# Pre, post, F1 and F2 of a fused attention and feed-forward kernel moved into two 64-row tiles of TensorE, where QK already runs

## The chip, the cores and the metric

One core of a Trainium2 chip. Times are device microseconds; quoted times are medians of the runs of one kernel. The profile is one execution with the hardware profiler on; its span is some microseconds shorter than the device time, as it runs from the first to the last instruction. Here a run is called slow when it took over 1.5% longer than the fastest of its kernel. Engines: PE is TensorE (PEld its weight loads), DVE is VectorE, ACT is ScalarE, POOL is GpSimd, SP is SyncE.

## The reference

```python
batch, n_heads, seq, head_dim = (8, 12, 448, 64)
n_tokens, d_model, d_ff = (3584, 768, 2048)

scores = scale * np.matmul(q, k.transpose(0, 1, 3, 2))           # QK
scores = np.einsum('bhij,hg->bgij', scores, w_pre)               # pre: mixes the 12 heads
scores = scores - np.max(scores, axis=-1, keepdims=True)
attn = np.exp(scores)
attn = attn / (np.sum(attn, axis=-1, keepdims=True) + 1e-09)
attn = np.einsum('bhij,hg->bgij', attn, w_post)                  # post: mixes the heads again
out = np.matmul(attn, v)                                         # AV
x = out.transpose(0, 2, 1, 3).reshape(3584, 768)
h = np.maximum(x @ w_in, 0.0)                                    # F1
return h * h @ w_out                                             # F2
```

## The kernel before

The kernel is a program that plans itself: when it is built, a list scheduler walks over "units" of TensorE work (T, the transposes of q and k; QK, pre, post, AV, F1, F2), picks the next one by priority among those whose inputs and banks of PSUM (TensorE's output memory) are free by durations written into the code, and assigns the copies out of PSUM to ACT or DVE. What comes out is a fixed order for each engine with semaphore waits between them. On the chip nothing is chosen any more.

The heads are mixed in chunks of 10 query positions x 12 heads = 120 rows. `pre` multiplies a chunk of scores by a block-diagonal 120 x 120 matrix; ACT takes exp; `post` multiplies by the block-diagonal matrix of `w_post`, whose rows are first scaled by one over the row sum (reciprocal on DVE, "fold" on POOL).

```python
# pre: one matmul, K = 120, one bank
eng.matmul(ps[0:128, bank, 0:S], wk1[:, :], dring[:, slot, :], start=True, stop=True)

# post: four matmuls of 120 columns, K = 120, one bank
for jb in range(RJ):
    eng.matmul(ps[0:128, bank, jb * NR:(jb + 1) * NR],
               pring[:, pr, jb * JB:jb * JB + 128], wk2s[:, ws, :], start=True, stop=True)
# ... the copy out: runs of CH = 10 elements
src = ps[0:JB, bank, 0:RJ * NR].rearrange("p (a k n) -> p a k n", a=RJ, k=H)
return copy(eng, en, a2t[half][:, :, :, cs * CH:(cs + 1) * CH], src)

# F1: a chain of 6 matmuls, K = 128, into one bank; F2 likewise with 16
for ft in range(f0, f0 + 3):
    eng.matmul(ps[:, bank, 0:n], w_in_sb[:, ft, t16 * 128:(t16 + 1) * 128],
               xt[:, ft, c0:c1], start=(ft == 0), stop=(ft == NFT - 1))

# priorities of the units (lower goes first): AV 1, post 2, pre 3, QK 4, T 5, F1 6, F2 7
```

QK alone runs in two 64-row tiles at once: TensorE's 128 rows are used as two halves, each with weights and a matmul of its own (here two heads of 64 dimensions, each into its own bank). There are 8 PSUM banks. F1 of a batch needs that batch's AV and the F2 of the batch before; F2 needs all of F1. So F work is the filler between pieces of attention work.

The softmax here doesn't subtract the row's maximum and nothing guards it: scores larger than these inputs give would overflow.

## Time and profile before

| | before |
|---|---|
| time | 600.76 us (600.68 to 600.85, 2 runs) |
| span of the profile, granted clock | 595.2 us, 0.999 |
| matmuls | 6024 |
| busy PE, ACT, DVE, POOL | 98, 75, 59, 58% |
| PE runs out of inputs | about 10 us in all |

Three more lines of the page of the kernel before matter later: the two groups of copies of post's output (DVE and ACT; busy us, then the mean ns of one; the column after that is idle time before them), and the granted clock in 40 slices (9 is 90% or more).

```profile
L388 DVE CAST a2t<-ps 112x480 bf16<-112x480 f32 x195 | 124.7, 650 | 45.5 <-PE ps L877 43.6
L387 ACT ACTIVATE a2t<-ps 112x480 bf16<-112x480 f32 x165 | 92.6, 576 | 24.5 <-PE ps L877 22.6
```

```profile
PEclk9999999999999999999999999999999999999999
```

### The profile page before, as it was taken

The page shows a single profiled execution, that of the slowest core. Times are in us where ns is not written, and L with a number is a line of the kernel's source. Part 1 is how long each engine was busy: PE and PEld are TensorE (multiplying, and loading weights), DVE is VectorE, ACT ScalarE, POOL GpSimd, SP SyncE. Part 2 cuts the span into 40 slices and gives each one's busy share as a digit, 9 for nine tenths or more (in the row PEclk, how much of TensorE's full clock was granted, in tenths as well). Part 3 has the DMA queues.
Part 4 walks back from the last instruction along what each step waited for, and adds up shares of the span by engine and source line. Part 5 has one row for each costly group of instructions (what it writes and reads, how often), then busy time and mean ns, then how long its engine had stood idle before and what let it go on. Part 6 is the DMA issues. An engine that isn't in the chain of part 4 may idle for free.

```text
span 595.2 us, 15926 instructions
## 1 busy us (share of the span) xinstructions
PE 580.4 (98%) x6024; PEld 377.4 (63%) x6024; DVE 351.5 (59%) x899; ACT 446.4 (75%) x1160; POOL 342.3 (58%) x684
## 2 busy tenths in 40 slices
PE   7989999999999999999999999999999999999997
PEld 3656766685876565656556655657555665566974
DVE  4778775587666755754768655765647535230420
ACT  2779577888777979797977797889788867772531
POOL 8786758377692657645764566474367534761001
PEclk9999999999999999999999999999999999999999
DMA  9999879577886986459744896447544565301103
GB/s 135 184 225 214 141 132 202 114 144 116 153 135 129 180 157 133 88 91 170 162 88 72 163 183 146 77 81 124 132 100 81 91 116 131 82 2 49 34 26 80
DMA packets 95851, 72.40 MB, mean 122 GB/s; under 512 B 6192, under 2 KB 93440, under 8 KB 95776
## 3 DMA queue, kind: packets, MB, share of 16 engines
q0 software_dynamic: 49504, 33.43, 36.5%
q1 hardware_dynamic: 46128, 37.85, 29.1%
q8 instruction: 49, 0.80, 0.5%
q14 instruction: 26, 0.21, 0.1%
q10 hardware_dynamic: 144, 0.10, 0.1%
HBM read 45.70 MB, written 11.01 MB: 95 GB/s over the span
## 4 chain that ended last, share of the span: by engine, by line
PE 88%; ACT 3%; DMA 3%; DVE 2%; POOL 1%; SPq 1%; issue 1%; ACTq 0%; POOLq 0%
PE ps L1080 24%; PE ps L998 24%; PE ps L877 12%; PE ps L813 11%; PE ps L939 7%; PE ps L738 7%; PE ps L612 3%; ACT stage L387 2%; DMA dring<-stage 2%; DMA kraw<-in_k_dram 1%; SPq L785 1%; ACT pring L831 1%; DVE w_out_sb L656 1%; DVE stage L388 1%; DVE a2t L388 0%
## 5 line engine op out<-in xcount | busy, mean ns | idle before, releaser
L831 ACT ACTIVATE pring<-ps 120x448 bf16<-120x448 f32 x360 | 191.2, 557 | 15.9 <-PE ps L813 13.1
L847 POOL TENSOR_SCALAR wk2s<-wk2b,rinv 120x120 bf16<-120x120 bf16 x350 | 125.1, 367 | 84.4 <-DVE rinv L841 81.7
L998 PE MATMUL ps<-xt,w_in_sb 128*128 128x448 bf16 (+6 forms) x1248 | 173.4, 281 | 0.2 <-DVE h1t L1027 0.2
L1080 PE MATMUL ps<-w_out_sb,h2t 128*128 128x384 bf16 x896 | 165.1, 326 | 0.0
L388 DVE CAST a2t<-ps 112x480 bf16<-112x480 f32 x195 | 124.7, 650 | 45.5 <-PE ps L877 43.6
L1036 POOL TENSOR_TENSOR h2t<-h1t 128x448 bf16<-128x448 bf16 (+6 forms) x176 | 114.0, 661 | 43.7 <-ACT h1t L1026 23.6
L998 PEld LDWEIGHTS ps<-xt,w_in_sb 128*128 128x128 bf16 x1248 | 98.9, 97 | 41.1 <-issue 5.7
L877 PE MATMUL ps<-wk2s,pring 120*128 120x120 bf16 x1440 | 119.3, 216 | 1.6 <-POOL wk2s L847 0.5
L877 PEld LDWEIGHTS ps<-wk2s,pring 120*128 120x128 bf16 x1440 | 93.5, 97 | 42.3 <-POOL wk2s L847 5.0
L1080 PEld LDWEIGHTS ps<-w_out_sb,h2t 128*128 128x128 bf16 x896 | 83.3, 97 | 56.5 <-issue 6.3
L387 ACT ACTIVATE a2t<-ps 112x480 bf16<-112x480 f32 x165 | 92.6, 576 | 24.5 <-PE ps L877 22.6
L841 DVE RECIPROCAL rinv<-rowsum 120x1 f32<-120x1 f32 x360 | 53.3, 157 | 93.2 <-ACT pring L831 92.5
L387 ACT ACTIVATE stage<-ps 120x896 bf16<-120x896 f32 (+3 forms) x99 | 88.9, 918 | 23.5 <-PE ps L738 23.1
L388 DVE CAST stage<-ps 120x896 bf16<-120x896 f32 (+2 forms) x87 | 93.6, 1086 | 20.2 <-PE ps L738 19.4
L813 PE MATMUL ps<-dring,wk 120*128 120x448 bf16 x350 | 93.8, 353 | 2.8 <-ACT pring L831 1.6
L1141 POOL DMA_DIRECT2D out_dram<-osb x54 | 34.1, 634 | 84.1 <-ACT osb L387 72.1
L831 ACT ACTIVATION_READ_ACCUMULATOR pring<-ps 120x1 f32 x360 | 79.9, 222 | 0.0
L1027 DVE TENSOR_SCALAR h1t<-ps 128x448 bf16<-128x448 f32 (+6 forms) x111 | 43.7, 396 | 31.3 <-PE ps L998 25.0
L1026 ACT ACTIVATE h1t<-ps 128x448 bf16<-128x448 f32 (+5 forms) x97 | 42.7, 443 | 20.4 <-PE ps L998 19.7
L738 PE MATMUL ps<-qkt 64*128 64x448 bf16 (+2 forms) x372 | 54.7, 359 | 1.5 <-ACT stage L387 0.5
L813 PEld LDWEIGHTS ps<-dring,wk 120*128 120x128 bf16 x350 | 32.5, 97 | 27.0 <-ACT pring L831 2.9
L387 ACT ACTIVATE osb<-ps 128x384 f32<-128x384 f32 x35 | 17.2, 491 | 35.6 <-PE ps L1080 35.0
(41 smaller groups left out, 352.5 us busy)
## 6 DMA issues: line engine op xcount, KB each, us to landing
dring<-stage SPq DMA_DIRECT2D x342, 105.0 KB
vraw<-in_v_dram POOLq DMA_DIRECT2D x24, 224.0 KB, 6.0
qraw<-in_q_dram POOLq DMA_DIRECT2D x23, 224.0 KB, 6.4
kraw<-in_k_dram POOLq DMA_DIRECT2D x23, 224.0 KB, 7.9
w_in_sb<-in_moe_w_in_dram POOLq DMA_DIRECT2D x8, 384.0 KB, 10.7
w_out_sb<-in_moe_w_out_dram POOLq DMA_DIRECT2D x12, 256.0 KB, 33.2
out_dram<-osb POOLq DMA_DIRECT2D x8, 336.0 KB, 3.6
out_dram<-osb POOLq DMA_DIRECT2D x8, 288.0 KB, 4.2
```

Of the source, the lines that this page charges most:

```text
L387: return eng.activation(o, i_, AF.Copy)
L388: return eng.tensor_copy(o, i_)
L738: r_ = eng.matmul(ps[0:m, banks[par], 0:S], qkt[r0:r0 + 64, pb, p, 0, i0:i0 + m], qkt[r0:r0 + 64, pb, p, 1, :], start=True, stop=True,)
L813: return eng.matmul(ps[0:128, bank, 0:S], wk1[:, :], dring[:, slot, :], start=True, stop=True)
L831: return eng.activation(pring[:, pr, 0:S], ps[0:NR, bank, 0:S], AF.Exp, accum_out=rowsum[:, pr, :])
L841: return eng.reciprocal(rinv[:, pr, :], rowsum[:, pr, :])
L847: return eng.tensor_scalar(wk2s[:, ws, :], wk2b[:, :, :].rearrange("p a b -> p (a b)"), rinv[:, pr, :], 1.0, op0=ALU.mult, op1=ALU.mult)
L877: r_ = eng.matmul(ps[0:128, bank, jb * NR:(jb + 1) * NR], pring[:, pr, jb * JB:jb * JB + 128], wk2s[:, ws, :], start=True, stop=True,)
L998: r_ = eng.matmul(ps[:, bank, 0:n], w_in_sb[:, ft, t16 * 128:(t16 + 1) * 128], xt[:, ft, c0:c1], start=(ft == 0), stop=(ft == NFT - 1),)
L1027: return eng.tensor_scalar(h1t[:, s, 0:n], ps[:, bank, 0:n], 0.0, None, op0=ALU.max)
L1036: return eng.tensor_tensor(h2t[:, t16, o0:o0 + n], h1t[:, s, 0:n], h1t[:, s, 0:n], ALU.mult)
L1080: r_ = eng.matmul(ps[:, bank, 0:FH], h2t[:, t16, col:col + 128], w_out_sb[:, t16, hh * FH:(hh + 1) * FH], start=(t16 == 0), stop=(t16 == N ...
```

## The change

Its intent: when everything but T and AV runs in two 64-row tiles, (1) QK no longer forces a change of TensorE's tiling mode, and (2) post can use the block structure: the five query positions of a row tile reach 60 columns only, so a matmul pair streams 60 columns where one matmul streamed 120. The price: a product with K = 128 is now two halves on two row tiles. The change doesn't let them write one bank at the same time, so two outputs are made together: tile 0 fills bank A and tile 1 bank B with one half of K each, then they swap banks for the other half, with a wait of PE on itself between. Reciprocal and fold are done once for two chunks.

```diff
-        NPS = 6
-        NWS = 6
+        NPS = 8
+        PR = 60
@@ pre, two chunks at once
-                    return eng.matmul(ps[0:128, bank, 0:S], wk1[:, :], dring[:, slot, :],
-                                      start=True, stop=True)
+                    for y in range(2):
+                        x = ph ^ y
+                        ra, rb = (64, NR) if y else (0, 64)
+                        r_ = eng.matmul(ps[:, banks[x], 0:S], wk1[ra:rb, :],
+                                        dring[ra:rb, gs[x] % NDS, :],
+                                        start=ph == 0, stop=ph == 1)
+                if ph:
+                    t_pre.sync = deps
@@ post, two chunks at once
-                    for jb in range(RJ):
-                        r_ = eng.matmul(
-                            ps[0:128, bank, jb * NR:(jb + 1) * NR],
-                            pring[:, pr, jb * JB:jb * JB + 128],
-                            wk2s[:, ws, :],
+                    for y in range(n):
+                        for jb in range(RJ):
+                            o0 = (y * RJ + jb) * PR
+                            for x in range(2):
+                                r_ = eng.matmul(
+                                    ps[:, banks[x], o0:o0 + PR],
+                                    pring[64 * x:64 * x + PR, pr + y, jb * JB:jb * JB + 128],
+                                    wk2s[64 * x:64 * x + PR, pr + y, :],
@@ the copy out of post: two copies, runs of 5 elements
+                        src = ps[0:JB, banks[x], 0:n * RJ * PR].rearrange(
+                            "p (c q t) -> p c q t", c=n, t=CH // 2)
+                        d = a2t[half][:, :, :, cs * CH:(cs + n) * CH].rearrange(
+                            "p r h (c i) -> p c (r h) i", c=n)
+                        return copy(eng, en, d[:, :, :, x * (CH // 2):(x + 1) * (CH // 2)], src)
@@ F1 (F2 likewise)
-                    (box["bank"],), box["freed"] = take(1)
+                    box["banks"], freed = take(2, True)
+                    chains["open"] += 1
...
                     for ft in range(f0, f0 + 3):
-                        r_ = eng.matmul(
-                            ps[:, bank, 0:n],
-                            w_in_sb[:, ft, t16 * 128:(t16 + 1) * 128],
-                            xt[:, ft, c0:c1],
+                        for y in range(2):
+                            x = ph ^ y
+                            t = t16 + x
+                            r_ = eng.matmul(
+                                ps[:, banks[x], 0:n],
+                                w_in_sb[64 * y:64 * y + 64, ft, t * 128:(t + 1) * 128],
+                                xt[64 * y:64 * y + 64, ft, c0:c1],
...
+                if ph and f0 == 0:
+                    t.sync = [box["t"]]
```

(Cut: the masks and weights laid out for 60 + 60 rows, the direct scores of the first ten chunks padded to 128 columns, changes in the planner: banks need not be neighbours, F1 and F2 come as two streams of which one chain is open at a time, and offsets for priorities, margins and pacing through a table `TABLE` that is empty.)

## The prediction

> **What bounds the kernel now.** I read the page's busy table first, then the waits of TensorE (PE), the costliest groups by shape, and PE's timeline at a few places.
>
> ```profile
> PE 580.4 (98%) x6024; PEld 377.4 (63%) x6024; DVE 351.5 (59%) x899; ACT 446.4 (75%) x1160; POOL 342.3 (58%) x684
> PE 88%; ACT 3%; DMA 3%; DVE 2%; POOL 1%; SPq 1%; issue 1%; ACTq 0%; POOLq 0%
> ```
>
> PE is busy 98% of the span and is 88% of the chain that ended last (second line). But busy marks overlap (a matmul's mark lasts past the start of the next), so 98% doesn't say that PE streams all the time. The waits of PE are the check:
>
> ```profile
> PE ps L813 <- ACT pring L831: 1.6, 2, 1.3
> PE ps L577 <- DVE warm L562: 1.5, 1, 1.5
> PE ps L685 <- DVE w_out_sb L656: 1.4, 2, 0.7
> ```
>
> The lines give total us, times, longest; all of PE's waits together are about 10 us, most in the first 60 us. So PE bounds the time, and what counts is the distance from one matmul's start to the next. The timeline gives it for post and narrow F1, the chain of waits for the end (start, length of the merged run, what, count):
>
> ```profile
> 303.76 0.58 PE L877 MATMUL ps<-wk2s,pring 120*128 120x120 bf16 x8
> 58.28 4.18 PE L998 MATMUL ps<-xt,w_in_sb 128*128 128x100 bf16 x91
> ```
>
> ```profile
> 552.40 18.40 PE ps L998 x192
> 570.81 20.81 PE ps L1080 x128
> ```
>
> Eight post matmuls of 120 columns: (0.58 - 0.216)/7 = 52 ns each. F1 with 100 columns: (4.18 - 0.21)/90 = 44 ns. F1 at 230 and 218 columns: 18.40/192 = 96 ns; F2 at 384 columns: 20.81/128 = 162.6 ns. All are columns/2.4 + 2.5 ns: PE runs at its column rate, a new weight load ahead of every matmul included. Summing that rule over all matmuls in the trace (QK, the transposes and AV count half, as they already run two at a time) gives 541 us. The start-to-start distances sum to 590 us. Of the 49 us between, this place shows the largest item:
>
> ```profile
> 204.75 0.81 PE L1080 MATMUL ps<-w_out_sb,h2t 128*128 128x384 bf16 x4
> 205.50 0.74 PE L738 MATMUL ps<-qkt 64*128 64x448 bf16 x6
> 206.17 0.38 PE L877 MATMUL ps<-wk2s,pring 120*128 120x120 bf16 x4
> ```
>
> Four F2 matmuls need 4 x 162.6 = 650 ns, so QK could start at 205.40; it starts at 205.50. Its three pairs: (0.74 - 0.36)/2 = 190 ns a pair, so two 64-row matmuls of 448 columns cost what one 128-row matmul costs (189). Post could start at 205.50 + 0.57 = 206.07; it starts at 206.17. Entering and leaving the two-row-tile mode costs about 100 ns each. In order of start, QK's pairs form 102 runs in the trace and the transposes and AV 29; the excess over the column rule at the mode changes sums to 21 us for QK and 8.8 us for the others. The remaining 19 us are waits and late starts, two thirds before 60 us.
>
> **What the Trainium skill says.** (1) "TensorEngine Tiling (Array Packing)", Tiling Modes, Key Properties: changing the tiling mode, not the tile, drains TensorE. The trace agrees: 95 to 100 ns a change. (2) Same page, Restrictions and Gotchas, Gotcha 1: different row tiles cannot access the same PSUM bank simultaneously and software must synchronize. No run here shows it, but it explains why the change needs a wait at each swap. (3) "TensorE: Matmul & The Clock Gate", Part 1, "Wait - 56ns, not 53.3ns?": start to start is N/2.4 + about 2.5 ns, with a floor near 25 ns however small N is. The trace agrees down to 100 columns; nothing in it is shorter for one tile, so 60 columns (27.5 ns) is an extrapolation close to that floor. (4) Same page, Back-to-back issue gap: a stream of weight load and matmul pairs is put at about 81 ns at N=128. The trace differs: 52 ns at 120 columns with a load for each. I use the trace.
>
> **The change part by part.**
>
> *Post.* The mixing matrix of 10 rows x 12 heads is block diagonal, so the rows of the first five query positions only reach 60 of the 120 output columns. Before, 1440 matmuls stream 120 columns each. After, each becomes a pair on the two row tiles that streams 60 columns to two banks: 60/2.4 + 2.5 = 27.5 ns if both loads hide. In QK's runs the loads of the two tiles start 3 to 4 ns apart and the next pair of loads some 15 ns after the first, so I take 29 ns. 1440 x (52.5 - 29) = -34 us, all on PE.
>
> *QK's mode changes.* Post, pre, F1 and F2 now also run in 64-row tiles, so QK no longer changes mode: about 100 runs x (95 + 100 ns) = -19.5 us. The direct scores of the first ten chunks and the warming matmuls stay full, and meet row-tile work in the first 30 us: perhaps ten runs x 2 x 95 ns = +2 us. Transposes and AV keep their changes.
>
> *Pre, F1, F2 as pairs.* Pre's 350 matmuls, F1's 1248 and F2's 896 each become a pair of half-K matmuls for two outputs at once. By QK's 190 ns a pair costs one old matmul: 0. Even the narrow F1 of 100 columns has 44 ns for two loads that need about 15.
>
> *Swaps.* A bank gets its first half of K from one row tile and its second from the other, so the second phase waits for PE's own semaphore. 104 pairs of F1 outputs (13 column groups x 8), 28 F2 tiles, 175 pre pairs: 307 swaps. From the start of a pre matmul to the start of the exp that it releases takes 386 to 392 ns when the exp waits for nothing else. A second phase with no work between would start that late instead of 189 ns later: 200 ns lost. The planner counts this latency and puts other units there (a pre or QK pair is 190 ns, a post unit 8 x 29 = 230). I let one in nine be exposed: 307/9 x 0.2 = +7 us. All exposed would be +61 us.
>
> *PSUM.* F1, F2, pre and post now take two banks at a time of eight, F for a whole chain. Bank time per chunk, estimated from the rows (pre to exp start 0.39, exp 0.56, copies 0.58 to 1.09 us): before about 0.95 pre + 1.05 post + 1.45 QK + 2.15 F + 0.35 AV = 5.9 bank-us per 1.65 us, or 3.6 banks; after 1.8 + 1.1 + 1.45 + 3.6 + 0.35 = 8.3 per 1.55 us, or 5.3 banks. Tighter, not full: +5 us.
>
> *Other engines.* Reciprocal and fold are done once for two chunks:
>
> ```profile
> L847 POOL TENSOR_SCALAR wk2s<-wk2b,rinv 120x120 bf16<-120x120 bf16 x350 | 125.1, 367 | 84.4 <-DVE rinv L841 81.7
> L841 DVE RECIPROCAL rinv<-rowsum 120x1 f32<-120x1 f32 x360 | 53.3, 157 | 93.2 <-ACT pring L831 92.5
> L831 ACT ACTIVATE pring<-ps 120x448 bf16<-120x448 f32 x360 | 191.2, 557 | 15.9 <-PE ps L813 13.1
> ```
>
> DVE loses 180 x 157 = 28 us of work, POOL about 175 x 367 = 60 us (it multiplies as many elements per partition for two chunks as for one before). Neither is on the chain, so 0. Exp and the copies keep their counts of elements per partition.
>
> *Where PE isn't the bound.* In the first 60 us DMA is saturated (digits of 9, then 8 and 7) and ACT, DVE and loads pace PE; 132 post matmuls lie there, worth 132 x 23.5 = 3 us, which I take as not gained: +3. At the end both halves of the last output tile now finish together and are stored together: +1.
>
> Sum: -34 - 19.5 + 2 + 7 + 5 + 3 + 1 = -35.5 us; 600.8 - 35.5 = **565 us**.
>
> **The rivals.**
> 1. *The weight loads bound post.* Two loads and two matmuls per 28 ns is a rate that nothing in the trace shows over a stretch: the transposes need four instructions per 49 ns. For: the 25 ns floor if it holds per instruction and not per tile, which gives 50 ns a pair and no gain. Against: two tiles' matmuls start 3 to 4 ns apart. At 40 ns a pair the time is about 581, at 52 ns about 599.
> 2. *The swap waits take the place of the mode changes.* For: three times as many swaps as QK runs, each dearer. Against: other work fits nearly everywhere before the last 60 us, and there two chains can take turns. A third exposed: +13, about 579.
> 3. *ACT or the PSUM banks become the bound.* From 200 to 500 us ACT is busy 83% and DVE 63%. If this stretch shrinks by a tenth, the same work makes ACT 92%; but copies may move to DVE, which loses reciprocals. The mean is then near 78%, with two banks freed one after another. For: exp is fixed on ACT, 0.78 us a chunk with its accumulator read. If it stalls PE for 5% of the middle: +15, about 580.
> 4. *Fewer stalls than I charge.* POOL's shorter fold releases post earlier and eight slots replace six: about 552.
>
> **Range and chances.** The gains (53 us) rest on durations measured in this trace except post's 29 ns. The charges (18 us) could be half or double, and 40 ns for post would cost 16 more. Two misfortunes together give about 584; few stalls give 548. Range 548 to 584. 2% is 588.8: to stay above it, post must gain almost nothing or most swaps be exposed. Faster 0.91, within 2% 0.07, slower 0.02.
>
> **What would show it.** Post: start-to-start of its pairs near 29 ns; at 40 to 52 rival 1 holds. QK: next to pre, post or F at 189 ns, not 285. F1 and F2 pairs: 189 and 162 ns; anything above would cost 2144 times that and break the "0" above. Swaps: PE waiting on PE in the waits, below 10 us in all. Banks: PE's waits on the copies (stage, a2t, h1t) and exp, now 4 us, below some 10. POOL's fold busy near 65 us. I'm wrong if row-tile pairs lose their overlap outside QK, if the swap costs more than 200 ns, or if the attention part falls behind and leaves PE without filler in the middle.

## The result, and the profile after

The changed kernel takes 650.14 us (650.13 to 650.15, 2 runs): slower by 8.2% (ratio 1.0822, 95% interval 1.0775 to 1.0868). A second set of runs on another occasion gave 650.18 us and 1.0867. Ratios here are the mean time of one kernel's fast runs over the mean of the other's of the same rounds, so not quite the ratio of the medians quoted. On that second occasion, and in all experiments below, the kernel before took 597.5 to 598.9 us.

First the page of the changed kernel: busy times, the chain that ended last by engine, and the clock.

```profile
PE 576.7 (89%) x9961; PEld 368.1 (57%) x9961; DVE 359.1 (55%) x756; ACT 450.1 (69%) x1139; POOL 284.1 (44%) x512
...
PEclk9998898889998997999999989899989998999999
...
PE 65%; DMA 9%; ACT 9%; DVE 6%; issue 4%; SPq 4%; POOL 2%; POOLq 0%
```

PE has more matmuls (9961) and is busy 89% in place of 98%. In the chain it falls from 88% to 65%: DMA, ACT and DVE have become links. And the clock row, all 9 before, shows dips: the mean granted clock is 0.961.

What PE does is as quick as foreseen. Its timeline in a full stretch:

```profile
226.48 0.35 PE L889 MATMUL ps<-dring,wk 64*128 64x448 bf16 x2
...
226.67 0.55 PE L800 MATMUL ps<-qkt 64*128 64x448 bf16 x4
...
227.05 1.47 PE L1206 MATMUL ps<-w_out_sb,h2t 64*128 64x384 bf16 x16
...
228.35 0.39 PE L972 MATMUL ps<-wk2s,pring 60*128 60x60 bf16 x16
```

A pre pair, then QK after 190 ns, then F2 after two QK pairs at 2 x 190 ns: no mode change. Eight F2 pairs: (1.47 - 0.33)/7 = 163 ns a pair. Eight post pairs, whose 16 matmuls start about evenly (15 steps, or 7.5 pairs): (0.39 - 0.19)/7.5 = 27 ns a pair, four instructions each.

What is new are the waits, of PE and of its weight loads (total us, times, longest):

```profile
PE ps L889 <- DMA dring<-stage: 18.1, 13, 2.8
PE ps L1111 <- issue: 10.0, 5, 3.0
PE ps L889 <- ACT pring L914: 5.5, 8, 1.4
```

```profile
PEld ps L889 <- PE ps L889: 20.9, 57, 0.5
PEld ps L1111 <- issue: 13.3, 18, 3.2
PEld ps L889 <- ACT pring L914: 13.0, 17, 2.8
PEld ps L889 <- DVE rinv L925: 8.7, 4, 2.4
```

The first line of the second view is the swap: 57 of the 175 pre pairs wait on PE itself, 0.37 us each. "issue" means that PE waited for nothing that the profile shows; more on it below. The rest are inputs that come late.

Where they come late is seen in a stretch without F work, from the end of F2 of one batch at 237 us to the start of F1 of the next at 258.56 (PE, 22 us of 648):

```profile
241.06 0.40 PE L972 MATMUL ps<-wk2s,pring 60*128 60x60 bf16 x16 [0.26 <-ACT pring L914]
241.77 0.70 PE L800 MATMUL ps<-qkt 64*128 64x448 bf16 x4 [0.31 <-DVE stage L411]
242.79 0.40 PE L972 MATMUL ps<-wk2s,pring 60*128 60x60 bf16 x16 [0.32 <-ACT a2t L410]
243.77 0.40 PE L972 MATMUL ps<-wk2s,pring 60*128 60x60 bf16 x16 [0.59 <-ACT pring L914]
244.41 0.79 PE L889 MATMUL ps<-dring,wk 64*128 64x448 bf16 x4 [0.24 <-issue]
245.03 0.54 PE L800 MATMUL ps<-qkt 64*128 64x448 bf16 x4
247.60 1.17 PE L889 MATMUL ps<-dring,wk 64*128 64x448 bf16 x4 [2.02 <-DMA dring<-stage]
```

The chain that ended last has this piece for the transfer behind the last gap:

```profile
239.40 7.95 DMA dring<-stage
```

Nearly every unit waits: for exp (L914), for a copy that must empty a bank (stage L411, a2t L410), and last for scores that DMA regroups (stage to dring). That transfer was issued at 239.40 and took 7.95 us. Regrouping as such didn't get slower: from issue to the last semaphore update the median of its 350 transfers is 4.7 us, 5.0 in the kernel before. From 239 to 244.8 us ACT goes from one instruction to the next. In the gap of 2 us, at 246.0 us, the clock falls: a pre pair of L889 at 247.60 takes longer than before (4 matmuls in 1.17 us, 0.79 at 244.41).

To add it all up I went through the trace and took, for each matmul (each pair once), the distance to the next one's start, less columns/2.4 + 2.5 ns. What is left is "late", sorted by the semaphore that the next weight load waits for; in stretches at half clock the doubled streaming is put aside first. The sorting by semaphore takes waits of several engines for that of the one named, so the rows of lateness are rough; the sums are not. Waits for the regrouping DMA (18.1 us of PE in the view above) have no row of their own. Nor is the row of streaming the column rule alone: with every row-tile matmul counted half, the rule gives 541 us before and 506 after, so 35 us less where the row has 29.

| us | before | after | after, reordered | post alone, reordered |
|---|---|---|---|---|
| streaming | 540 | 511 | 511 | 507 |
| mode changes | 24.5 | 7.1 | 7.0 | 40.5 |
| late behind ACT and DVE | 13 | 57 | 47 | 9 |
| late behind PE itself (swaps) | 0 | 23 | 11 | 0 |
| out of instructions | 0 | 11 | 8 | 2 |
| half clock | 0 | 17 | 2 | 3 |
| everything else | 12 | 15 | 9 | 12 |
| first to last matmul | 590 | 642 | 594 | 574 |

(The last two columns are experiments, below.) In the changed kernel 14 stretches of over 4 us without an F matmul make up 116 us, and 54 of 115 us late (counted after the first F matmul, clock and mode changes included) lie in them. Before there were 13 such stretches, 72 us, with 8 of 33 us late. So about half of the new loss falls where PE has no F work, and the other half beside F work.

Two more things on the page changed. The copies of post's output take longer for the same 480 elements, ACT 755 ns (576), DVE 728 ns (650):

```profile
L411 DVE CAST a2t<-ps 112x480 bf16<-112x480 f32 x205 | 143.0, 728 | 58.1 <-PE ps L972 57.0
L410 ACT ACTIVATE a2t<-ps 112x480 bf16<-112x480 f32 x139 | 100.2, 755 | 37.4 <-PE ps L972 36.7
```

And in the first 130 us there are five gaps of 2 to 3.2 us (from one matmul's start to the next) before which PE waits for nothing. One of them, with the engines' busy times in three windows around it (the last columns are granted clock, DMA share, GB/s):

```profile
50.42 0.34 PE L1111 MATMUL ps<-xt,w_in_sb 64*128 64x130 bf16 x6
53.75 0.34 PE L1111 MATMUL ps<-xt,w_in_sb 64*128 64x130 bf16 x6 [2.99 <-issue]
```

```profile
50.00:53.00 3.00, 0.76 (x22) 0.41 (x16) 0.16 (x1) 1.31 (x5) 1.03 (x3) 1.00 1.37 221
...
55.00:58.00 3.00, 3.00 (x66) 2.51 (x64) 1.80 (x7) 2.38 (x9) 2.10 (x7) 0.50 1.36 212
```

The gap falls in the middle of one chain, between two instructions that wait for nothing. F1 runs here with 130 columns, four instructions per 57 ns, while the DMA engines are full (1.37). The trace records the DMA queue that brings instructions: 80 blocks of 16 KB (49 before), and one of them starts at 51.3 us, inside the gap; the other four gaps each have one too, from 0.5 us before the last matmul's start to 0.8 us after it. From 54.9 to 58.3 us the clock is then at a half.

### The profile page after: what moved, and what is told of

The parts are those of the page before. It is cut to its first block, busy times and chain, and to the rows that moved or that the text cites. A ratio compares the mean times of both kernels' runs of the same rounds, so it can differ in the third digit from the quotient of the medians.

```text
span 648.4 us, 23470 instructions
## 1 busy us (share of the span) xinstructions
PE 576.7 (89%) x9961; PEld 368.1 (57%) x9961; DVE 359.1 (55%) x756; ACT 450.1 (69%) x1139; POOL 284.1 (44%) x512
## 4 chain that ended last, share of the span: by engine, by line
PE 65%; DMA 9%; ACT 9%; DVE 6%; issue 4%; SPq 4%; POOL 2%; POOLq 0%
PE ps L1111 20%; PE ps L1206 19%; PE ps L889 9%; DMA dring<-stage 9%; PE ps L1040 6%; PE ps L972 5%; ACT pring L914 4%; SPq L847 4%; PE ps L800 3%; PE ps L667 3%; ACT a2t L410 2%; DVE a2t L411 2%; ACT stage L410 2%; DVE w_out_sb L718 1%; DVE stage L411 1%
## 5 line engine op out<-in xcount | busy, mean ns | idle before, releaser
L914 ACT ACTIVATE pring<-ps 128x448 bf16<-128x448 f32 x360 | 191.9, 551 | 46.9 <-PE ps L889 43.5
L1111 PE MATMUL ps<-xt,w_in_sb 64*128 64x448 bf16 (+6 forms) x2496 | 188.5, 285 | 12.3 <-issue 10.0
L411 DVE CAST a2t<-ps 112x480 bf16<-112x480 f32 (+1 forms) x226 | 151.1, 701 | 61.8 <-PE ps L972 60.5
L1206 PE MATMUL ps<-w_out_sb,h2t 64*128 64x384 bf16 x1792 | 173.7, 326 | 2.4 <-ACT a2t L410 1.2
L889 PE MATMUL ps<-dring,wk 64*128 64x448 bf16 (+1 forms) x700 | 126.6, 366 | 31.4 <-DMA dring<-stage 18.1
L1111 PEld LDWEIGHTS ps<-xt,w_in_sb 64*128 64x128 bf16 x2496 | 107.0, 97 | 60.0 <-issue 13.3
L410 ACT ACTIVATE a2t<-ps 112x480 bf16<-112x480 f32 (+1 forms) x150 | 104.7, 734 | 39.0 <-PE ps L972 38.4
L1206 PEld LDWEIGHTS ps<-w_out_sb,h2t 64*128 64x128 bf16 x1792 | 89.5, 95 | 55.9 <-PE ps L1206 2.8
L410 ACT ACTIVATE stage<-ps 120x896 bf16<-120x896 f32 (+3 forms) x101 | 91.3, 920 | 27.4 <-PE ps L800 26.3
L411 DVE CAST stage<-ps 120x896 bf16<-120x896 f32 (+2 forms) x85 | 91.6, 1083 | 29.6 <-PE ps L800 29.1
L972 PE MATMUL ps<-wk2s,pring 60*128 60x60 bf16 x2880 | 73.0, 191 | 10.1 <-issue 3.5
L889 PEld LDWEIGHTS ps<-dring,wk 64*128 64x128 bf16 (+1 forms) x700 | 36.6, 95 | 73.4 <-PE ps L889 20.9
L914 ACT ACTIVATION_READ_ACCUMULATOR pring<-ps 128x1 f32 x360 | 77.0, 214 | 0.0
```

Source lines behind the costliest of these rows:

```text
L410: return eng.activation(o, i_, AF.Copy)
L411: return eng.tensor_copy(o, i_)
L889: r_ = eng.matmul(ps[:, banks[x], 0:S], wk1[ra:rb, :], dring[ra:rb, gs[x] % NDS, :], start=ph == 0, stop=ph == 1)
L914: return eng.activation(pring[:, pr, 0:S], ps[:, bank, 0:S], AF.Exp, accum_out=rowsum[:, pr, :])
L972: r_ = eng.matmul(ps[:, banks[x], o0:o0 + PR], pring[64 * x:64 * x + PR, pr + y, jb * JB:jb * JB + 128], wk2s[64 * x:64 * x + PR, pr + y, ...
L1111: r_ = eng.matmul(ps[:, banks[x], 0:n], w_in_sb[64 * y:64 * y + 64, ft, t * 128:(t + 1) * 128], xt[64 * y:64 * y + 64, ft, c0:c1], start=( ...
```

## The experiments

The theories after the first look. **A**: PE's streaming still sets the time and something in it is dearer than I measured. **B**: PE's work is less, but the inputs and banks it needs come late, because units hold two banks and the copies take longer. **C**: the waits of the swaps. **D**: the supply of instructions and the clock. **E**: the order that the planner gave.

### e1_post_stretched: give the saving of post back

Same order, same results; each post matmul streams its 60 columns twice.

```diff
-                                    ps[:, banks[x], o0:o0 + PR],
+                                    ps[:, banks[x], o0:o0 + m * PR],
                                     pring[64 * x:64 * x + PR, pr + y, jb * JB:jb * JB + 128],
-                                    wk2s[64 * x:64 * x + PR, pr + y, :],
+                                    rhs.to_broadcast([PR, m, PR]),   # m = 2, the last one 1
```

> The changed kernel in its own order, with each post matmul streaming its 60 columns twice (the second copy is overwritten by the next matmul or left unused), so post costs about 1260 pairs x 25 ns = 31.5 us more of TensorE streaming; instructions, copies and results stay. If TensorE's streaming still sets the time, it rises by 28 to 33 us over the changed kernel's 650. If PSUM banks and the engines that empty them set it, the stretched post fills time in which TensorE waits anyway: it rises by 0 to 15 us.

650.84 us (fast runs 647.49 to 652.41; a fourth, slow, took 660.43), ratio 1.0865. The changed kernel itself had 1.0822 and 1.0867. PE's busy time rose by 16 us, to 592.8, and 32 us of streaming were absorbed: in the trace the time late behind ACT and DVE fell from 57 to 44 us and the loss at half clock from 17 to 7. A falls: what post saves on PE is worth nothing in this order.

### e2_no_swap: take the swap waits away

Same order; in phase 1 each tile stays with its bank, so no wait is needed. The result is wrong.

```diff
-                            x = ph ^ y
+                            x = y
...
-                if ph and f0 == 0:
-                    t.sync = [box["t"]]
```

> Wrong result on purpose: in the second phase each row tile stays with its bank, so TensorE needn't wait for itself; order and all other work as in the changed kernel. In the trace of the changed kernel 95 late starts behind a wait on TensorE's own semaphore cost 23 us. If these are lost one for one, 650 falls to 622 to 630 (more if the clock recovers, 17 us of loss lie there). If the banks bound the time, most of it turns into waits for banks: 638 to 650.

642.75 us (637.35 to 646.77), ratio 1.0711. Against the changed kernel (1.0867) that is 1.5%, some 9 us of the 23: inside the second expectation, that of the banks. The waits on PE itself are gone from the trace (23 to 0 us), and those behind ACT and DVE rose from 57 to 69. C holds in part only; more than half of it turns into waits for inputs and banks.

### e3_wide_runs: copies with runs of 10 elements

Same order; each copy writes 480 elements as 48 runs of 10 in place of 96 runs of 5. The result is wrong.

```diff
-                            "p (c q t) -> p c q t", c=n, t=CH // 2)
+                            "p (q t) -> p q t", t=CH)
...
-                        return copy(eng, en, d[:, :, :, x * (CH // 2):(x + 1) * (CH // 2)], src)
+                        return copy(eng, en, d, src)     # one chunk's columns, runs of CH
```

> Wrong result on purpose: the copies of post's output write runs of 10 elements (20 bytes) as before and not of 5; the same number of elements, order as in the changed kernel. Theory: the 5-element runs made these copies longer (ACT 573 to 755 ns, DVE 648 to 728 ns), so they go back to about 573 and 648, and the time falls by 10 to 25 us because banks come free earlier. Rival: the copies are longer for another reason (a longer access pattern, ACT and DVE together at the port) and stay near 755 and 728; the time stays.

640.15 us (638.49 to 642.04), ratio 1.0698: 1.6%, some 10 us less. The groups by shape:

```profile
L411 DVE CAST a2t<-ps 112x480 bf16<-112x480 f32 x205 | 128.8, 650 | 57.5 <-PE ps L972 56.8
...
L410 ACT ACTIVATE a2t<-ps 112x480 bf16<-112x480 f32 x139 | 77.3, 580 | 32.4 <-PE ps L972 31.7
```

Both are back at the durations of before. The edit also takes a dimension out of the access pattern, which is the rival. The copies of a single chunk settle it: there that dimension has size one in both versions, and their 240 elements in runs of 5 took 464 ns on ACT and 437 on DVE, in runs of 10 here 374 and 399, half of the difference for half of the runs. So the runs of 5 elements (10 bytes) cost 175 ns a copy on ACT and 78 on DVE, and that alone costs 10 us. This edit changes no instruction of PE: the time follows the engines that empty the banks.

### e5_before_narrow_split: is it the supply of instructions?

The kernel before with the F1 matmuls of the first batch cut into two column halves (384 matmuls more). No row tiles, no waits on itself.

```diff
+                    if b == 0:
+                        s0, s1 = (0, n // 2) if f0 == 0 else (n // 2, n)
+                        fts = range(NFT)
...
-                            ps[:, bank, 0:n],
+                            ps[:, bank, s0:s1],
```

> The kernel before, with the F1 matmuls of the first batch alone (130, 100, 110, 108 columns) cut into two column halves: 384 more matmuls, the same result. TensorE's streaming grows by 384 x 2.5 = 1 us. Theory: gaps of 2 to 3 us that nothing explains, seen in the changed kernel between 43 and 75 us when F1's narrow matmuls run, are TensorE running out of instructions while the DMA queues are full: then 2 to 4 such gaps appear here too, 4 to 10 us, with half clock after them. Rival: they belong to row tiles or to the self-waits: then 601 to 603 us and no such gaps.

603.78 us (597.03 to 605.9), ratio 1.007 (1.0007 to 1.0132): 0.7%, some 5 us, and one of the four runs lost nothing. PE's timeline of the profiled run, the longest of the four, and the clock after the second gap:

```profile
58.32 1.14 PE L1003 MATMUL ps<-xt,w_in_sb 128*128 128x50 bf16 x39
61.44 3.38 PE L1003 MATMUL ps<-xt,w_in_sb 128*128 128x50 bf16 x128 [1.98 <-issue]
67.91 0.66 PE L1003 MATMUL ps<-xt,w_in_sb 128*128 128x50 bf16 x13 [3.09 <-issue]
```

```profile
68.00:71.40 3.40, 3.40 (x32) 2.00 (x33) 1.32 (x5) 2.20 (x8) 1.05 (x4) 0.50 0.91 123
```

The gaps appear in the kernel before as soon as its narrow matmuls are halved, again with a block of instructions on its way (59.0 and 65.6 us) and half clock after the second. So it is shown that the gaps need neither row tiles nor waits of PE on itself, only many short matmuls in this stretch. That PE runs out of instructions there is inferred from the block of instructions at every one of the seven gaps; no run changes the supply itself. The gaps are worth some 11 us in the changed kernel, plus part of the clock.

### e6_after_7banks and e7_before_7banks: how much hangs on the banks?

One line in each: `NB = 8` becomes `NB = 7`. The planner orders anew.

> The changed kernel planned for 7 PSUM banks in place of 8; the planner orders anew, the work is the same. If banks bound the changed kernel, taking one away costs much: 685 to 720 us (35 to 70 more; the kernel's own planner says 49 more). If its loss is in the swap waits, the instruction supply or the clock, one bank less costs little: under 665.

> The kernel before planned for 7 banks. If it has banks to spare, as I took for granted, it loses little: 602 to 612 us (its planner says 14 more). If every kernel of this kind hangs on its banks, it loses as much as the changed one, 635 or more, and banks don't tell the two apart.

The changed kernel: 681.33 us (676.91 to 685.12), ratio 1.1389, so 5.2 points, 31 us, over itself with 8 banks. The kernel before: 623.54 us (621.65 to 624.66), ratio 1.042, 25 us more. My first expectation was nearly met (just under its low end), the second missed: the kernel before has no bank to spare either. Banks bind both kernels, the changed one somewhat more; the pair doesn't separate B from the rest as cleanly as I had hoped. As each was ordered anew, part of either loss may be the order's. But the prediction took for granted that 3.6 banks of 8 in use on average left room, and in the order the planner finds they didn't.

### u1_F_whole: undo one part

F1 and F2 as before (whole, one bank, no swap); QK, pre and post stay in row tiles, under a mode of their own.

```diff
-                        for y in range(2):
-                            x = ph ^ y
-                            t = t16 + x
-                            r_ = eng.matmul(
-                                ps[:, banks[x], 0:n],
+                        r_ = eng.matmul(
+                            ps[:, bank, 0:n],
...
-                           c_row(1, S), 0)                       # QK; pre and post likewise
+                           c_row(1, S), 0, "rows")
```

> One part undone: F1 and F2 again whole (128 rows, one bank a chain, no swap, half the instructions); QK, pre and post stay in row tiles, so mode changes between F and the rest come back. Bank and supply theory: TensorE no longer runs out of instructions near 45 to 75 us, waits on ACT and DVE fall from 56 us to under 40, mode changes rise from 7 to over 30 us: 610 to 635 us. Rival, that the 60-column post or the pre pairs alone do the harm: it stays at 645 or more.

631.06 us (629.76 to 633.14), ratio 1.0555. Mode changes cost 59 us in its trace (7 before the undoing), and yet it is 19 us faster: late behind ACT and DVE 26 us in place of 57, swaps 5 in place of 23, half clock 5 in place of 17, supply 1 in place of 11. So the paired F chains cost about 70 us (19 + 52 of mode changes), an estimate, as the planner ordered u1 anew.

### u3_post_rows: one part alone

Only QK (as ever) and post in row tiles; pre whole as well. It is u1 with the kernel before's `unit_pre` put back.

> One part alone: only QK (as ever) and post run in row tiles, post with 60 columns; pre, F1 and F2 whole, one bank each, no swap at all. Theory: the gain on TensorE in post is real (27 ns a pair), and what spoils it are the paired chains; then this gives 588 to 602 us, near or below the kernel before, with mode changes near 40 us in place of 24 and streaming near 510. Rival, that the post pairs themselves (their two banks and longer copies) do the harm: 620 or more.

601.5 us (601.28 to 608.43), ratio 1.0085. Streaming is 507 us, mode changes 47, no swaps. So post's 60 columns alone, untuned, give back in mode changes (47 against 24.5 us) and in longer copies what they save in streaming (33 us): about even. From u1 to u3, undoing pre's pairs gave 30 us more, of which 12 are mode changes (59 to 47). So in the orders that the untuned planner finds, the paired chains make the change a loss: F's some 70 us and pre's some 18 with mode changes put aside.

### e4_after_reordered: the same instructions in another order

Theory E. The planner of the changed kernel is told the measured duration of the copies, and its empty table is filled with priorities by batch, margins and pacing, found by trying some thousands of them for a short plan that bears late copies and late DMA. The plan is arithmetic with the durations in the code, not a time of the chip.

```diff
-TABLE = {}
+TABLE = {'F1': (-1.43, -2.18, -3.18, -4.46, -4.75, -2.91, -3.53, -3.23),
+         'F2': (-3.07, -5.56, -5.88, -4.99, -5.82, -3.23, -5.7, 0.4),
+         'post': (3.21, 3.11, 2.25, 1.36, 3.3, 1.04, 3.46, 1.08), ...}
...
-                               [t_post, av_of.get((b - 1, half))], c_ev(n * RJ * PR),
+                               [t_post, av_of.get((b - 1, half))],
+                               {ACT: (n * RJ * PR / 1.2 + 65.0 + 92 * n, ...
```

> The changed kernel with the same instructions in another order: its planner gets the measured length of post's copies and another set of priorities, margins and pacing, found by searching for a short plan that bears late copies. Theory: much of the loss is order, as TensorE's work is 35 us less than before but runs dry of F work and meets full banks; then 605 to 630 us. If order isn't it and banks, self-waits, instruction supply and clock cost what they cost in any order, it stays at 640 or more. If the order were all, it would fall below 590.

602.32 and 594.75 us in its two fast runs, ratio 1.0014 (0.9932 to 1.0095), and correct; two more, slow, took 603.9 and 604.01. That is beyond the better end of what I expected for a large part of the loss, but not under 590. The same matmuls (and five warming ones more), copies (16 of them moved from ACT to DVE) and swaps, in another order, take 8.5 points or some 51 us less. The table of lateness above shows where: half clock 17 to 2, swaps 23 to 11, behind ACT and DVE 57 to 47. Stretches without F work fell from 116 to 68 us. The clock row of its page:

```profile
PEclk9999999999999999999999999999999999999999
```

The offsets show what the order does: F moves ahead of post (on average F1 6 - 3.2 = 2.8, post 2 + 2.4 = 4.4), so attention becomes the filler, and F work runs out for less of the time.

### v1_post_rows_reordered and v0_before_reordered: a better version, and its control

The u3 version and the kernel before, each given the same kind of search.

> The version with post and QK alone in row tiles, ordered anew in the same way (it had 601.5 in the untuned order). Its plan is 17 us shorter than the untuned one: 578 to 592 us, faster than the kernel before by 1 to 3%. If the order found by the planner doesn't carry over to the chip: 598 to 606.

> Control: the kernel before, ordered anew by the same search. If its order was already as good as such a search gets: 592 to 600 us. Its plan is 8 us shorter: 587 to 596. If it falls as much as the two others, the gain of those belongs to the search and not to the row tiles.

The u3 version reordered: **581.74 us** (579.2 to 585.02), ratio 0.9736 (0.969 to 0.9781), correct: faster than both kernels. The kernel before reordered: 601.76 us (598.59 to 604.94), ratio 1.0067: the search, which promised 8 us in its plan, gave nothing on the chip (a miss: I expected 587 to 600). So the 2.6% do not come from searching alone; with the same kind of search the version with post in row tiles is 3.3% faster than the one without (0.9736/1.0067). It takes both: without the search the same version stood at 1.0085. And it differs from the kernel before in more than post's tiles (fold for two chunks, eight slots, banks that need not be neighbours), so the 3.3% belong to the whole. Its page and its waits:

```profile
PE 562.9 (97%) x7468; PEld 340.0 (59%) x7468; DVE 356.3 (62%) x751; ACT 446.4 (77%) x1144; POOL 285.4 (49%) x512
```

```profile
PE ps L683 <- DMA kraw<-in_k_dram: 2.1, 1, 2.1
PE ps L898 <- DMA dring<-stage: 1.7, 4, 0.7
PE ps L1102 <- issue: 1.5, 1, 1.5
```

PE is busy 97% again and hardly waits.

### e0_after_again

The changed kernel unedited beside e4, v0 and v1.

> The changed kernel itself, unedited, beside the others on one chip: 640 to 655 us, ratio to the kernel before 1.07 to 1.09, with a spread of some us between runs[...].

650.18 us (647.37 to 651.6), ratio 1.0867. As expected; it is the base for the percentages of the experiments above, which ran beside the kernel before only.

## Why the prediction was wrong

Said: 565 us, 548 to 584. Measured: 650. Point by point.

- **What bounds the kernel before: right, but read one step short.** PE's streaming does set its time. But at 98% PE it had no slack in its banks: planned for 7 it loses 25 us.
- **Post, -34 us: right on PE.** 27 ns a pair (29 assumed), and the column rule's sum fell by 35 us. e1 shows that this was worth nothing in the order given.
- **QK's mode changes, -17.5 us net: right.** 24.5 to 7.1 us (the prediction counted 29.8 for the kernel before).
- **Pairs cost what one matmul costs: right** (163 and 190 ns).
- **Swaps, +7 us: too low.** 95 late starts, 23 us (0.24 us each, 0.2 assumed), where I let one in nine of 307, or 34, be exposed. By e2 they are worth some 9 us; the rest would be lost to other waits anyway.
- **"Tighter, not full: +5 us" (PSUM): this step failed.** I worked out a mean occupancy of banks (5.3 of 8) and took the distance from 8 for slack. The time late behind ACT and DVE rose by 44 us. A better order doesn't cure this: in e4 it is still 47 us against 13 before, so 34 us more where 5 were allowed, and that is the largest part of what keeps e4 from 565. A mean says nothing of the stretches in which F has run out and PE waits for exp and copies, as from 240 to 245 us above.
- **"The planner ... puts other units there": this step failed too, and it is the larger half.** I took the order for good because the order of before is good. The order is made anew from the durations in the code with the priorities of the kernel before, and filler runs out: e4, with the same work, is at 1.0014 of the kernel before, where the changed kernel is at 1.0867. I named the danger at the very end ("if the attention part falls behind and leaves PE without filler in the middle") and gave it no number; rivals 2 and 3 together were worth some 28 us (13 + 15), which gives 593, and I put "two misfortunes together" at 584.
- **"Exp and the copies keep their counts of elements": true, and the durations of the copies did not keep.** Runs of 5 elements cost 175 and 78 ns a copy, 10 us of the time (e3). Elements were counted, the run length was not looked at.
- **Not foreseen: the supply of instructions (11 us) and the clock (17 us).** That such gaps need no row tiles is shown by e5. The second goes with the idle time: with the order mended it is 2 us. In e2 and e3, where the gaps stay, it stays too (15 and 16 us). That idle time is its cause is argued.

What stays open: how the 85 us between prediction and result divide among banks, copies, swaps and supply exactly. They feed each other (e2: a wait removed comes back as another), and e6 and e7 didn't separate the banks from the rest. That the order is the largest lever is shown; that the first order is bad because of the low priority of F is argued from the offsets and from the stretches without F work, not tried one offset at a time.

## What to carry to other kernels

When an engine at 98% is given less work, ask first what it will wait for and what will fill the time: list what each unit now holds (banks, slots) and for how long, in the worst stretch and not on average. A kernel with a fixed order must be ordered anew and tuned after such a change before the change can be judged; here the same work took 650 or about 599 us. And take the part of a change that pays (60-column post) without the part that costs (chains in pairs with swaps): that gave 582.

## What the Trainium skill lacked or had wrong

- "TensorEngine Tiling (Array Packing)", Tiling Modes, Key Properties: says that a change of tiling mode drains TensorE, without a size. Here each costs 95 to 100 ns (499 of them 47 us in u3).
- Same page, Restrictions and Gotchas, Gotcha 1, names the pressure on PSUM but gives no cost of the swap that follows for K over 64. Here an exposed swap has the weight load wait 0.37 us (57 times in pre, 20.9 us).
- "TensorE: Matmul & The Clock Gate", Part 2, Back-to-back issue gap: about 81 ns a matmul at N = 128 with a load for each. The runs show 52 ns at 120 columns in one tile, and 27 ns for a pair at 60 columns in two row tiles with two loads.
- Same page, Why this matters for your kernels: advises against PE-idle gaps over about 3 us. Here half clock came in a gap of 2.0 us (from 245.6 us), after a stretch of shorter waits: from 246.0 us, for 6.8 us. At 143.6 and 413.3 us half clock followed several gaps of under 1 us. But a gap of 2.4 us that ended at 73.9 us in e4 was followed by full clock, so a gap's length alone doesn't tell. In all 17 us were lost so.
- "Runtime: NRT & Kernel Launch", Instruction fetch mechanics: calls the cost of crossing a 16 KiB boundary "mostly hidden". With four TensorE instructions per 57 ns beside busy DMA engines it was, by all signs, not: five gaps of 2.0 to 3.2 us from start to start, each with a block of instructions on its way, and two in e5 of 2.2 and 3.3 us.
- Pages speak of short runs in general, but none that I found has a figure for copies from PSUM to SBUF that write bf16 in short runs: 480 fp32 to bf16 took ACT 755 ns and DVE 728 ns in runs of 10 bytes, 580 and 650 ns in runs of 20 bytes.
